# 78 products that nobody reads, at the head of an attention kernel: 36 and 42 beside TensorE's first transpositions

## The chip, the cores and the metric

The kernel runs on one core of a Trainium2 chip. The metric is the device time of one execution in microseconds; lower is better. Engines are called by their short names: PE is TensorE, DVE VectorE, ACT ScalarE, POOL GpSimd, SP the queue that issues most transfers.

## The reference, cut to what matters

Three layers in a row: block-causal attention, a top-1 mixture of experts with a capacity, and a noisy top-2 mixture of experts. Only the attention is touched.

```python
def _attn_ref(q, k, v):                      # 2 batches, 8 heads, 576 tokens, 64 wide
    scores = scale * np.matmul(q, k.transpose(0, 1, 3, 2))
    scores = np.where(mask, scores, -1e9)    # block_i >= block_j, blocks of 64
    attn = np.exp(scores - scores.max(-1, keepdims=True))
    attn = attn / (attn.sum(-1, keepdims=True) + 1e-09)
    return np.matmul(attn, v)

def reference(q, k, v, ...):
    x = rows_of(_attn_ref(q, k, v))          # 1152 x 512
    x = _moe_ref(x, ...)
    return _moe2_ref(x, ...)
```

## The kernel before, in words

The attention works on pairs of heads: 8 pairs `pr`, four for each batch. For a pair, `load_pair` (L319 to L324) brings q, k and v into SBUF; for the first pair q comes through SP's queue and k through ACT's. `turn_ops` then builds `w`, the transposed operand of the scores, in the tiles `both`. It has three parts:

- `main(x)`, once for q (`x == 0`) and once for k (`x == 1`): four transpositions on PE into one PSUM bank of the ring `tp` (L442), two ACT copies that round to fp32r (L450), and two DVE operations that keep the rest (L456 for q, L459 for k).
- `tail()`: the last 64 tokens of q and k by one product with a scaled identity (L479), two ACT copies (L487) and two DVE operations (L492).
- `dup`: copies to the other half of the partitions. For the first pair q's is done by ACT (L468) and k's by POOL (L470).

`tile_ops` follows: the scores (L526, L531) into the ring `s`, their maxima on DVE (L537, L540, L542), the exponentials on ACT (L550, L552), transpositions of the probabilities on PE (L562, L558, L565), copies back on ACT or DVE (L421, L423) and the products with v (L608, L623) into the bank `av`. At the head, DVE also copies the first pair's masks into the second pair's tile (L876).

Nothing of this is issued in the order in which it is written. `AT`, a `Weave`, collects operations with an engine, a cost and their dependences, and `run` simulates the engines with the costs given and issues each operation's instructions in the order that comes out. A function `pe(op)` is called when its operation's turn comes, so whatever it issues stands together in PE's queue, in front of whatever comes later. Each engine works through its own queue in order. The constant `ones` is a 128x128 bf16 tile that DVE sets to 1.0 at the program's start (L88); the attention's gates use it much later.

Of the kernel before, what the change touches and what calls it, by code (L numbers as in the profile page):

```python
# [46 lines left out]
def attention_moe_moe2(ctx, tc, q, k, v, wg1, w1a, w2a, cap, wg2, wn2, noise, w1b, w2b, out):  # L47
    nc = tc.nc
# [38 lines left out]
    ones = consts.tile([128, 128], BF, name="ones")  # L87
# [118 lines left out]
    class Weave:  # L206
# [80 lines left out]
        def bank(self, op, ring):  # L287
            return self.rings[ring][op["bank"][ring]]
# [8 lines left out]
    with ExitStack() as actx:  # L297
# [16 lines left out]
        def load_pair(b, p):  # L314
            qn, q4, vn = qns[(b * NP + p) % 2], q4s[(b * NP + p) % 2], vns[(b * NP + p) % 3]
            hs = slice(2 * p, 2 * p + 2)
            for i, src in enumerate((q, k)):
                for hh in range(2):
                    (nc.scalar if b == p == 0 and i == 1 else nc.sync).dma_start(out=qn[:, i, :, hh, :], in_=src[b, 2 * p + hh, 0:512, :].rearrange("(c p) d -> p c d", p=128))  # L319
            for i, src in enumerate((q, k)):  # L320
                nc.sync.dma_start(out=q4[64 * i:64 * i + 64], in_=src[b, hs, 512:576, :].rearrange("h p d -> p h d"))
            for hh in range(2):
                nc.sync.dma_start(out=vn[:, hh, 0:4, :], in_=v[b, 2 * p + hh, 0:512, :].rearrange("(c p) d -> p c d", p=128))
            nc.sync.dma_start(out=vn[0:64, :, 4, :], in_=v[b, hs, 512:576, :].rearrange("h p d -> p h d"))  # L324
# [78 lines left out]
        def store(b, c):  # L403
# [6 lines left out]
        rings = dict(s=pairs, big=big, p4=[P4], av=[psum.tile([128, 512], F32, name=f"av{i}") for i in range(RING["av"])],  # L410
                     tp=[psum.tile([128, 512], F32, name=f"tp{i}") for i in range(RING["tp"])],
                     pt=[work.tile([128, 512], F32, name=f"pt{i}") for i in range(RING["pt"])],
                     pT=[work.tile([128, 512], F32, name=f"pT{i}") for i in range(RING["pT"])],
                     xt=[work.tile([128, S], F32, name=f"xt{i}") for i in range(RING["xt"])])
# [9 lines left out]

        made = {}

        def load_op(pr):
            b, p = divmod(pr, NP)
            deps = [made.get(("tr", pr - 2, x)) for x in range(3)] + [made.get(("av", pr - 3))]
            made["load", pr] = AT.add("load", "S", 0.5, lambda op: load_pair(b, p), deps, dma=4.9)  # L430

        def turn_ops(pr):

            qn, q4, w = qns[pr % 2], q4s[pr % 2], W[pr % 2]
            used = made.get(("scores", pr - 2))
            res = []

            def main(x):
                C = [slice(64 * x * h, 64 * x * h + 512) for h in range(2)]
                def pe(op):  # L440
                    for t in range(4):
                        nc.tensor.transpose(bank(op, "tp")[:, 128 * t:128 * t + 128], qn[:, x, t].rearrange("p h d -> p (h d)"), ident)  # L442

                P = AT.add("tr", "P", 0.53, pe, [made["load", pr], used], ["tp"], shared=["tp"])
                made["tr", pr, x] = P

                def act(op):
                    for h in range(2):
                        o, c = HALF[h], C[h]
                        nc.scalar.activation(w[o, 2 * x, h, c], bank(P, "tp")[o], AF.Copy, scale=(0.125, 1.0)[x])  # L450

                def dve(op):
                    for h in range(2):
                        o, z, c = HALF[h], HALF[1 - h], C[h]
                        if x == 0:
                            nc.vector.scalar_tensor_tensor(w[z, 1, h, c], bank(P, "tp")[o], 0.125, w[o, 0, h, c].bitcast(F32),  # L456
                                                           op0=OP.mult, op1=OP.subtract)
                        else:
                            nc.vector.tensor_tensor(w[z, 2, h, c], bank(P, "tp")[o], w[o, 2, h, c].bitcast(F32), op=OP.subtract)  # L459

                def dup(op):
                    for h in range(2):
                        o, z = HALF[h], HALF[1 - h]
                        d = slice(0, 640) if x == 0 else slice(64 * h, 64 * h + S)
                        if pr:
                            nc.sync.dma_start(out=w[z, (0, 3)[x], h, d].bitcast(F32), in_=w[o, 2 * x, h, d].bitcast(F32))
                        elif x == 0:
                            nc.scalar.activation(w[z, 0, h], w[o, 0, h].bitcast(F32), AF.Copy)  # L468
                        else:
                            nc.gpsimd.tensor_copy(w[z, 3, h, d], w[o, 2, h, d].bitcast(F32))  # L470

                A = AT.add("hi", "A", 1.17, act, [P])
                V = AT.add("lo", "V", 1.4, dve, [P, A], frees=[(P, "tp")])
                res.extend([A, V])
                return dup, A

            def tail():
                def pe(op):
                    nc.tensor.matmul(bank(op, "tp")[:, 0:128], q4.rearrange("p h d -> p (h d)"), eighth, start=True, stop=True)  # L479

                P = AT.add("tr", "P", 0.26, pe, [made["load", pr], used], ["tp"], shared=["tp"])
                made["tr", pr, 2] = P

                def act(op):
                    for h in range(2):
                        o, c = HALF[h], TAIL[h]
                        nc.scalar.activation(w[o, 0:3:2, h, c], bank(P, "tp")[o, 0:128].rearrange("p (x n) -> p x n", x=2), AF.Copy)  # L487

                def dve(op):
                    for h in range(2):  # L490
                        o, z, c = HALF[h], HALF[1 - h], TAIL[h]
                        nc.vector.tensor_tensor(w[z, 1:3, h, c], bank(P, "tp")[o, 0:128].rearrange("p (x n) -> p x n", x=2),  # L492
                                                w[o, 0:3:2, h, c].bitcast(F32), op=OP.subtract)

                A = AT.add("hi", "A", 0.55, act, [P])
                V = AT.add("lo", "V", 0.6, dve, [P, A], frees=[(P, "tp")])
                res.extend([A, V])
                return A

            a2 = tail()  # L500
            for x in range(2):
                dup, A = main(x)
                if pr:
                    res.append(AT.add("dup", "G", 2.08, dup, [A, a2], dma=0.9))
                else:
                    res.append(AT.add("dup", "AG"[x], (1.48, 1.8)[x], dup, [A, a2]))
            made["W", pr] = res
# [362 lines left out]
        made["load", 0] = AT.add("load", "S", 0.0, lambda op: None, dma=6.0, lag=-3.6)  # L870
        turn_ops(0)
        load_op(1)
        def masks(h):
            o = HALF[h]
# [29 lines left out]
        for i in range(MORE):  # L904
            pr = B * NP - 2 + i
# [14 lines left out]
    rings = {n: [pp.tile([128, 512], F32, name=f"{n}{i}") for i in range(c)] for n, c in (("y", 2), ("h", 2), ("tp", 2), ("sm", 2))}  # L920
# [81 lines left out]
    def prep(F, rows, n, x, c0, deps=(), when=0.0, more=None):  # L1002

        xh, xl = x
        h = {}

        def tr(bank):
            h["tp"] = bank.rearrange("p (k n) -> p k n", n=128)
            for kk in range(KD):
                k = slice(kk * 128, (kk + 1) * 128)  # L1010
                if more:
                    nc.tensor.matmul(h["tp"][:, kk, :], rows()[:, k], ident, start=True, stop=False)
                    nc.tensor.matmul(h["tp"][:, kk, :], more[0][:, k], more[1], start=False, stop=True)
                else:
                    nc.tensor.transpose(h["tp"][:, kk, :n], rows()[:n, k], ident[:n, :n])  # L1015

        def hi():
            nc.scalar.activation(xh[:, :, c0:c0 + n], h["tp"][:, :, :n], AF.Copy)  # L1018

        def lo():  # L1020
            nc.vector.tensor_tensor(xl[:, :, c0:c0 + n], h["tp"][:, :, :n], xh[:, :, c0:c0 + n].bitcast(F32), op=OP.subtract)  # L1021

        t = F.add("P", 1.7 if more else 0.43 if n > 64 else 0.12, tr, deps, take="tp", after=when)
        a = F.add("A", 0.48 if n > 64 else 0.2, hi, [t])
        l = F.add("V", 0.6 if n > 64 else 0.2, lo, [a], frees=t, tail=F.par["prep"])
        return (l, t) if more else l
# [740 lines left out]
    x, t = prep(F, lambda: G[0, "early"][2], 128, xT[0], 128, deps=[d, m], more=(end[0], perm))  # L1767
# [47 lines left out]
```

## Time and profile before

| what | value |
|---|---|
| median of 3 runs | 550.33 us (548.28 to 551.72) |
| the profiled execution's own time | 548.57 us |
| its span, first to last instruction | 546.9 us |
| PE busy over the span | 514.3 us (94%) |
| DVE, ACT, POOL busy over the span | 378.8, 293.9, 139.7 us |
| PE busy in the first of 40 slices (13.7 us each) | 3 tenths; 9 tenths in most others |

1.7 us of the profiled execution's time lie outside its span. All times in the rows further below are counted from the span's start. In a timeline, instructions of one kind that follow each other are merged: the row has the start of the first, the time to the end of the last and their count. An idle time stands in brackets with what ended it, where there was any.

### The profile page before, as it was taken

What the parts mean: (1) busy time and instruction counts of PE and PEld (TensorE: products, weight loads), DVE (VectorE), ACT (ScalarE), POOL (GpSimd) and SP (SyncE); (2) the same over time, 40 slices, a digit from 0 to 9 for tenths busy, and PEclk for the clock granted to TensorE, in tenths of its full rate; (3) what the DMA queues carried; (4) which work ended last, traced back from release to release, by engine and by line L of the source; (5) the groups of instructions that cost most, each with busy time, mean ns of one, the idle gap of its engine ahead of it and who ended that gap; (6) DMA issues with size and microseconds to landing.
All of it is one profiled execution on the core that took longest, in us unless ns stands there. A gap on an engine that the chain in (4) does not pass through costs nothing. (4 is left out here: it accounts for less than half of the span.)

```text
span 546.9 us, 10105 instructions
## 1 busy us (share of the span) xinstructions
PE 514.3 (94%) x3381; PEld 421.5 (77%) x3381; DVE 378.8 (69%) x1008; ACT 293.9 (54%) x580; POOL 139.7 (26%) x225
## 2 busy tenths in 40 slices
PE   3999999999879999999999998999999999999996
PEld 3778777778646876796975976888889797789794
DVE  7899988898649888757675567637657492657441
ACT  5888878981347776643443346335536171726130
POOL 3000000000362344313423224114415051455021
PEclk9999999999999999999999999999999999999999
DMA  6988895523457788854632444528585775286120
GB/s 135 229 220 231 233 241 157 167 78 106 143 164 269 248 261 286 272 176 136 202 121 86 124 157 144 175 96 288 197 305 163 253 257 181 80 311 191 65 67 36
DMA packets 71176, 99.17 MB, mean 181 GB/s; under 512 B 37130, under 2 KB 40586, under 8 KB 71088
## 3 DMA queue, kind: packets, MB, share of 16 engines
q1 hardware_dynamic: 63600, 83.16, 48.3%
q0 software_dynamic: 6432, 14.71, 8.9%
q8 instruction: 39, 0.64, 0.5%
q14 instruction: 49, 0.40, 0.3%
q10 hardware_dynamic: 1056, 0.26, 0.2%
HBM read 87.53 MB, written 12.25 MB: 182 GB/s over the span
## 5 line engine op out<-in xcount | busy, mean ns | idle before, releaser
L170 DVE TENSOR_TENSOR wl<-raw,wh 128x512 fp32r<-128x512 f32 x140 | 91.5, 685 | 11.7 <-ACT wh L167 11.4
L167 ACT ACTIVATE wh<-raw 128x1024 fp32r<-128x1024 f32 x70 | 71.1, 1052 | 19.9 <-PEq L1779 12.5
L170 DVE TENSOR_TENSOR both<-raw,both 128x512 fp32r<-128x512 f32 x100 | 66.0, 685 | 9.0 <-ACT both L167 8.6
L167 ACT ACTIVATE both<-raw 128x1024 fp32r<-128x1024 f32 x50 | 51.4, 1055 | 10.0 <-PEq L1779 8.3
L198 PE MATMUL h<-xh,wh 128*128 128x256 f32 (+1 forms) x184 | 53.0, 288 | 0.6
L199 PE MATMUL h<-xl,wh 128*128 128x256 f32 (+1 forms) x184 | 52.5, 286 | 0.0
L200 PE MATMUL h<-xh,wl 128*128 128x256 f32 (+1 forms) x184 | 52.3, 284 | 0.0
L1018 ACT ACTIVATE xh<-tp 128x512 fp32r<-128x512 f32 (+1 forms) x37 | 18.9, 536 | 56.3 <-PE tp L1015 54.6
L1586 POOL DMA_INDIRECT out_dram<-o,T2i x16 | 18.6, 1165 | 99.8 <-DVE o L1583 97.6
L1021 DVE TENSOR_TENSOR xl<-tp,xh 128x512 fp32r<-128x512 f32 (+1 forms) x37 | 21.8, 610 | 31.1 <-ACT xh L1018 28.4
L1145 ACT ACTIVATE hh<-h 128x512 fp32r<-128x512 f32 (+1 forms) x46 | 24.1, 523 | 34.9 <-PE h L200 22.7
L198 PE MATMUL h<-xh,both 128*128 128x256 f32 (+1 forms) x136 | 39.2, 288 | 2.5 <-DVE hl L1148 1.2
L1148 DVE SCALAR_TENSOR_TENSOR hl<-h,hh 128x512 fp32r<-128x512 f32 (+1 forms) x46 | 27.4, 596 | 19.8 <-ACT hh L1145 15.1
L199 PE MATMUL h<-xl,both 128*128 128x256 f32 (+1 forms) x136 | 39.0, 287 | 0.0
L200 PE MATMUL h<-xh,both 128*128 128x256 f32 (+1 forms) x136 | 38.8, 285 | 0.0
L198 PE MATMUL y<-wh,hh 128*128 128x512 f32 (+1 forms) x94 | 38.3, 408 | 0.0
L200 PE MATMUL y<-wh,hl 128*128 128x512 f32 (+1 forms) x94 | 37.0, 394 | 0.0
L199 PE MATMUL y<-wl,hh 128*128 128x512 f32 (+1 forms) x94 | 36.9, 393 | 0.0
L526 PE MATMUL s<-both 128*128 128x256 f32 (+2 forms) x128 | 33.2, 372 | 3.8 <-ACT both L468 2.5
L550 ACT ACTIVATE pt<-s,negmax 128x128 f32<-128x128 f32 (+3 forms) x64 | 33.3, 525 | 6.3 <-DVE negmax L537 5.1
L198 PEld LDWEIGHTS h<-xh,wh 128*128 128x128 f32 x184 | 34.6, 188 | 2.2 <-issue 1.6
L1437 POOL MEMSET xr<- 128x524 f32 x3 | 1.5, 547 | 131.5 <-DVE T1f L811 131.5
(295 smaller groups left out, 1327.4 us busy)
## 6 DMA issues: line engine op xcount, KB each, us to landing
raw<-in_moe_w_dram SPq DMA_DIRECT2D x120, 512.0 KB, 5.3
wf<-in_moe_w_dram SPq DMA_DIRECT2D x8, 512.0 KB, 5.6
out_dram<-zero SPq DMA_DIRECT2D x3, 768.0 KB, 5.5
both<-both SPq DMA_DIRECT2D x14, 160.0 KB, 2.6
raw<-in_q_dram SPq DMA_DIRECT2D x16, 128.0 KB, 3.4
vn<-in_v_dram SPq DMA_DIRECT2D x16, 128.0 KB, 2.5
both<-both SPq DMA_DIRECT2D x14, 144.0 KB, 3.1
raw<-in_k_dram SPq DMA_DIRECT2D x14, 128.0 KB, 3.5
```

The costliest lines, as they stand in the source:

```text
L167: nc.scalar.activation(h, t, AF.Copy)
L170: (nc.gpsimd if part == 3 else nc.vector).tensor_sub(l[:, c], t[:, c], h[:, c].bitcast(F32))
L198: nc.tensor.matmul(o, sh, mh, start=first, stop=False)
L199: nc.tensor.matmul(o, sh, ml, start=False, stop=False)
L200: nc.tensor.matmul(o, sl, mh, start=False, stop=last)
L526: nc.tensor.matmul(o, w[:, i, h, 128 * t:128 * t + 128], w[:, i + 2, h, 64 * h:64 * h + n], start=(i == 0), stop=(i == 1))
L550: nc.scalar.activation(o, i, AF.Exp, bias=negmax[:, pr, 2 * t + h:2 * t + h + 1], accum_out=ssum[b][:, t, 2 * p + h:2 * p + h + 1])
L1018: nc.scalar.activation(xh[:, :, c0:c0 + n], h["tp"][:, :, :n], AF.Copy)
L1021: nc.vector.tensor_tensor(xl[:, :, c0:c0 + n], h["tp"][:, :, :n], xh[:, :, c0:c0 + n].bitcast(F32), op=OP.subtract)
L1145: nc.scalar.activation(part(hfull[0], g - (KF - 2 * WHOLE) // per) if plain(g) else part(hh, g), of(g), AF.Relu)
L1148: nc.vector.scalar_tensor_tensor(part(hl, g), of(g), 0.0, part(hh, g).bitcast(F32), op0=OP.max, op1=OP.subtract)
L1586: ins = nc.gpsimd.indirect_dma_start(out=out, out_offset=_off(G[key][1][:n, 0:1]), in_=G[key, "o"][:n], in_offset=None, bounds_check=NT - ...
```

## The change

A helper issues n products of `ones` with `ones` (128x128, bf16) into the first 128 columns of the only `av` bank. Each starts and stops its own accumulation, and nothing reads the result before the first product with v overwrites it. 36 are issued in the operation of the first pair's `main(0)`, ahead of its transpositions, and 42 in the operation of the first pair's `tail`, behind its product. Costs and dependences that the `Weave` sees are unchanged.

```diff
         made = {}
 
+        def unread(n):
+            for _ in range(n):
+                nc.tensor.matmul(rings["av"][0][:, 0:128], ones, ones, start=True, stop=True)
+
...
             def main(x):
                 C = [slice(64 * x * h, 64 * x * h + 512) for h in range(2)]
                 def pe(op):
+                    if pr == x == 0:
+                        unread(36)
                     for t in range(4):
                         nc.tensor.transpose(bank(op, "tp")[:, 128 * t:128 * t + 128], qn[:, x, t].rearrange("p h d -> p (h d)"), ident)
...
             def tail():
                 def pe(op):
                     nc.tensor.matmul(bank(op, "tp")[:, 0:128], q4.rearrange("p h d -> p (h d)"), eighth, start=True, stop=True)
+                    if pr == 0:
+                        unread(42)
```

What this makes of the order, on PE at the attention's head. Before, with the semaphores that each row waits for (`raw_72` is the first pair's q and k, `tp_204`, `tp_205` and `tp_206` are the three banks of the ring `tp`, `q_128` the last 64 tokens; DMAHW marks a transfer):

```order
L442 MATMUL tp_204<-ident,raw_72 128x128 [waits DMAHW4_49,DMAHW2_49,DVE_49]
L442 MATMUL tp_204<-ident,raw_72 128x128 x3
L442 MATMUL tp_205<-ident,raw_72 128x128 [waits DMAHW1_49,DMAHW0_49]
L442 MATMUL tp_205<-ident,raw_72 128x128 x3
L479 MATMUL tp_206<-eighth,q_128 128x128 [waits DMAHW5_49,DMAHW3_49,DVE_49]
L526 MATMUL s_201<-both_106 128x256 [waits DVE_49,Activation_49]
L526 MATMUL s_201<-both_106 128x256 [waits DVE_49,Pool_49]
```

The four rows into `tp_204` are k's, the four into `tp_205` are q's: DVE's first operation on `tp_204` is k's (L459), its first on `tp_205` is q's (L456). After the change, at the same place (lines below the helper have moved by 6 to 8; of the repeated pairs of rows of L429 the first stands for the 36, the second for the 42):

```order
L448 MATMUL tp_204<-ident,raw_72 128x128 [waits DMAHW4_49,DMAHW2_49,DVE_49]
L448 MATMUL tp_204<-ident,raw_72 128x128 x3
L429 LDWEIGHTS ones
L429 MATMUL av_203<-ones 128x128
...
L448 MATMUL tp_205<-ident,raw_72 128x128 [waits DMAHW1_49,DMAHW0_49]
L448 MATMUL tp_205<-ident,raw_72 128x128 x3
L485 MATMUL tp_206<-eighth,q_128 128x128 [waits DMAHW5_49,DMAHW3_49,DVE_49]
L429 LDWEIGHTS ones
L429 MATMUL av_203<-ones 128x128
...
L534 MATMUL s_201<-both_106 128x256 [waits DVE_49,Activation_49]
```

The 36 stand behind k's four transpositions, which wait for a transfer, and in front of q's four. The 42 stand between the tail's product and the first scores. The rows of all other engines' queues are the same before and after.

## Rows read from the trace of the kernel before

**Rows 1.** Busy time of each engine by stretch (second number: its length; x: instructions).

```profile
core 0: us, PE busy (x) PEld busy (x) DVE busy (x) ACT busy (x) POOL busy (x), PEclk, DMA share, GB/s
7.83:10.35 2.52, 0.01 (x2) 0.01 (x1) 2.43 (x5) 2.38 (x6) 1.32 (x2) 1.00 0.90 205
10.35:13.50 3.15, 2.47 (x9) 1.99 (x9) 3.02 (x7) 1.51 (x5) 0.00 (x0) 1.00 0.55 125
13.50:17.33 3.83, 3.83 (x16) 3.73 (x17) 1.81 (x4) 2.68 (x9) 0.00 (x0) 1.00 0.73 165
21.30:30.00 8.70, 7.51 (x66) 5.61 (x65) 7.99 (x17) 8.54 (x17) 0.00 (x0) 1.00 1.03 242
30.00:60.00 30.00, 29.64 (x264) 23.58 (x262) 28.56 (x65) 26.13 (x76) 0.00 (x0) 1.00 0.87 242
```

**Rows 2.** PE's timeline, 5 to 35 us.

```profile
5.47 1.94 PE L442 MATMUL tp<-ident,raw 128*128 128x128 f32 x8 [5.47 <-DMA raw<-in_k_dram]
7.20 0.63 PE L479 MATMUL tp<-eighth,q 128*128 128x128 f32 x2
10.35 2.47 PE L526 MATMUL s<-both 128*128 128x256 f32 x8 [2.51 <-ACT both L468]
13.50 1.01 PE L526 MATMUL s<-both 128*128 128x384 f32 x2 [0.68 <-DVE both L876]
...
14.72 1.06 PE L442 MATMUL tp<-ident,raw 128*128 128x128 f32 x4
15.58 0.63 PE L479 MATMUL tp<-eighth,q 128*128 128x128 f32 x2
16.00 1.06 PE L562 MATMUL tp<-ident,pt 128*128 128x128 f32 x4
16.72 1.35 PE L526 MATMUL s<-both 128*128 128x384 f32 x4
17.90 0.50 PE L562 MATMUL tp<-ident,pt 128*128 128x128 f32 x3
...
31.02 0.60 PE L652 MATMUL tp<-ident,xt 128*128 128x128 f32 x4
```

**Rows 3.** ACT's timeline, 6 to 21 us.

```profile
6.59 1.19 ACT L450 ACTIVATE both<-tp 64x512 fp32r<-64x512 f32 x2 [1.95 <-PE tp L442]
7.87 0.57 ACT L487 ACTIVATE both<-tp 64x128 fp32r<-64x128 f32 x2
8.46 1.21 ACT L450 ACTIVATE both<-tp 64x512 fp32r<-64x512 f32 x2
9.57 1.48 ACT L468 ACTIVATE both<-both 64x640 fp32r<-64x640 f32 x2
...
16.25 0.55 ACT L487 ACTIVATE both<-tp 64x128 fp32r<-64x128 f32 x2 [0.37 <-PE tp L479]
...
18.30 0.58 ACT L550 ACTIVATE pt<-s,negmax 128x384 f32<-128x384 f32 x1 [0.28 <-DVE negmax L540]
...
20.35 1.21 ACT L450 ACTIVATE both<-tp 64x512 fp32r<-64x512 f32 x2 [0.33 <-PE tp L442]
```

**Rows 4.** DVE's timeline, 0 to 22 us.

```profile
0.97 0.17 DVE L88 MEMSET ones<- 128x128 bf16 x1 [0.97 <-PEq L1798]
...
9.86 1.41 DVE L456 SCALAR_TENSOR_TENSOR both<-tp,both 64x512 fp32r<-64x512 f32 x2
11.29 0.85 DVE L876 CAST both<-both 64x640 fp32r<-64x640 f32 x2
```

**Rows 5.** PE's timeline, 11.74 to 12.9 us: the last scores of the first two tiles.

```profile
11.48 1.33 PE L526 MATMUL s<-both 128*128 128x256 f32 x5
```

**Rows 6.** PE's timeline around 132.8 us: bf16 products of 48 columns.

```profile
132.80 0.26 PE L806 MATMUL tp<-where,place 128*128 128x48 bf16 x4
```

**Rows 7.** PE's timeline, 450 to 454 us: products of 512 columns, one row each.

```profile
449.91 0.39 PE L199 MATMUL y<-wl,hh 128*128 128x512 f32 x1
450.14 0.39 PE L200 MATMUL y<-wh,hl 128*128 128x512 f32 x1
```

## The prediction

> **What bounds the kernel now.** I read the stretches first, then PE's timeline at the head, then ACT's and DVE's. The reader is to see three things.
>
> First, at the head the engines wait for each other in a chain. PE transposes k and q from 5.47 and ends the tail's product at 7.20 + 0.63 = 7.83 [rows 2]. ACT takes the tail (L487) at 7.87, q at 8.46 and q's copy at 9.57, with hardly a gap, and the first scores start at 10.35 when that copy's first half is done [rows 2, 3]. In that gap PE does nothing (0.01 of 2.52 us) while ACT is busy for 2.38 [rows 1]. From 9.86 DVE has q's rest and the mask copies and is busy for 3.02 of the next 3.15 us from 10.35 [rows 1, 4].
>
> Second, PE runs at its lower level there. The page's granted clock says 1.00 in every stretch, but the durations say otherwise: four transpositions took 1.06 us at 14.72 and at 16.00, and 0.60 at 31.02; three took 0.50 at 17.90 [rows 2]. [...] Ahead of the rise PE had been busy without a gap for 3.83 us, from 13.50 [rows 1]; the 2.47 us busy from 10.35, which an idle stretch of 2.51 preceded and one of 0.68 followed, had brought no rise [rows 2].
>
> Third, behind the head the binding engine is ACT from 21.3 to 30 (8.54 of 8.70 us, PE 7.51), then PE (29.64 of 30.00 from 30 to 60) [rows 1]. No long idle time lies there in which a late head could vanish, so what the head loses or gains is passed on to the end, nearly one to one. PE as a whole is 94% busy.
>
> **The change part by part.** Only PE's queue changes. The two additions are priced one by one.
>
> *One unread product.* No row before has a 128-column bf16 product back to back. [...] I take 0.057 at the high and 0.11 at the low level. The weight load of each should not show: bf16 products of 48 columns, each with its load, fit four into 0.26 us, the last one's whole length included [rows 6]. Bounds: below, less than 0.07, which is 0.26 / 4; above, the 0.21 us from one fp32 transposition of 128 columns to the next at the low level, (7.20 - 5.47) / 8 [rows 2], and half of that at the high.
>
> [...]
>
> *The 36.* They don't stand in front of the first transpositions: k's four come first and wait for k's transfer until 5.47, so the 36 can't use the idle time before it. k's four are issued by 5.47 + 4 x 0.216 = 6.33; then q's four and the tail's product wait behind 36 x 0.11 = 3.96 us, at the low level. Behind the 36 stand, on PE, q's transpositions and the tail; on ACT L487, L450 for q and L468, in that order; on DVE L492, L456 and the mask copies; on POOL L470. All of them move. Only k's first copies (6.59 on ACT) and their rest on DVE stay.
>
> Against this, PE is then busy without a gap from 5.47, and I expect its clock to rise much earlier. By the one stretch that brought it, the earliest is 5.47 + 3.83 = 9.30. I place the rise at the end of the 36, about 10.3. q's transpositions and the tail then cost 0.60 + 2 x 0.11 = 0.81 us instead of 1.50 (6.33 to 7.83) [rows 2]. The tail is 3.96 - 0.69 = 3.27 us late. Bounds: a rise at 9.30 leaves 27 products at 0.11 and 9 at 0.057, and the tail is 2.8 late; one after only 2.47 us (7.94) leaves 2.1; one after q's transpositions leaves 3.96.
>
> [...]
>
> *The 42.* They fill the time in which ACT works. Their cover runs from the tail's last issue (7.20 + 2 x 0.21 = 7.62) to the first scores at 10.35: 2.73 us, moved as a whole. At the high level they take 42 x 0.057 = 2.4 us and cost nothing. At 0.11 they take 4.6 and cost 1.9. Their cover is gone from 2.73 / 42 = 0.065 us a product.
>
> *What the faster clock gives back.* Between 10.35 and 17.33 PE was busy for 2.47 + 3.83 = 6.3 us at the low level [rows 1]; at the high one that is 3.15 less. Not all of it lies on the path. Up to 16 us the path runs through DVE and ACT. After it ACT waited for PE's work three times: 0.37 at 16.25, 0.28 at 18.30 (DVE's maximum was behind a copy that waited for PE) and 0.33 at 20.35 [rows 3]; then ACT binds. With PE twice as fast these 0.98 us close, and no more, since an engine can't be earlier than its own work. Bounds: 0 and 3.15; I take 0.98, the nearest rows.
>
> *The sum.* 3.27 + 0 - 0.98 = +2.3 us. The profiled execution took 548.57 us (546.9 of span and 1.7 outside), so on its own base 550.9. The median of the three runs, 550.33, lies 1.8 above that execution; on it the sum is 552.6, and that is what I name, since medians are compared. It is 0.4% slower; a measurement of this kernel tells about 1% from no change.
>
> **Rivals.**
>
> 1. *All of PE's saved time counts.* For it: PE is 99% busy from 30 us on. Against: from 21.3 to 30 ACT is, and PE has idle time. Then 3.27 - 3.15 = +0.1: 550.4 us.
>
> 2. *An unread product takes twice as long, because its weight load is not hidden* (the slower side). For it: the fp32 transpositions of 128 columns stand 0.21 apart. Against: the 48-column products with their loads. With a rise at 9.30, 14 products at 0.213 and 22 at 0.11 end at 11.72, the tail at 12.53: 4.7 late; the 42 take 4.6 and stand out by 1.9; less 0.98 that is +5.6: 555.9 us, just over 1%. It decides from 0.065 us a product at the high level.
>
> 3. *The clock does not rise before the scores.* For it: I know of one rise, and busy time at 10.35 had brought none. Against: the 36 leave PE no gap. Then 3.96 + 1.9 and nothing given back: +5.9, 556.2 us.
>
> 4. *The change does what its title says, and the 36 run during the wait before 5.47.* `ones` is there from 0.97 + 0.17 = 1.14 [rows 4], so they would end at 1.14 + 3.96 = 5.1. k's copies would start 0.46 earlier and 0.98 be given back: 548.9 us. The order speaks against it.
>
> **How the numbers follow.** Forecast (a delay of 2.1 to 3.96, with 0.5 to 1.5 given back): 0.65, its own range 551.0 to 553.8. Rival 1: 0.15. Rival 2: 0.08. Rival 3: 0.08. Rival 4: 0.02. Something else: 0.02. The range takes in rival 1 less the spread of the runs (550.4 - 1.3 = 549.1) and rival 3 (556.2). Rivals 2 and 3 lie at the bound of 1%, about half beyond it: slower 0.09 with something else; faster 0.02; within 1% 0.89.
>
> **What would show it.** In the profile after: k's transpositions still at 5.47; 36 products behind them, 0.11 us apart, up to about 10.3; L495 on ACT (L487 before) at about 11.1 instead of 7.87; the 42 ended before the first scores, which start near 13.6; no transposition at the 1.06 length after it; ACT's idle times of 0.37, 0.28 and 0.33 gone; at 30 us and later everything some 2.3 us later. It would be wrong if the 42 end behind ACT's L474, if the first scores start before 12 or behind 15 us, or if the shift of 2 to 3 us is found at 30 us but not at the end.

## The result, and the profile after

The changed kernel takes 556.65 us (median of 6 runs, 554.41 to 561.26), the kernel before, on the same chip, 550.1 us (median of 6, 548.28 to 551.72). The ratio is 1.0124, with a 95% interval of [1.0086, 1.0162]; a ratio is taken over all runs and can differ by up to 0.2% from that of the medians. The forecast was 552.6, the range 549.1 to 556.2: the result lies 0.45 above the range, and beyond the 1% that tells from no change, where "slower" had a chance of 0.09.

The profiled execution took 556.87 us. From its page: the span, the clock in 40 slices, and the queue q8, named "instruction" (packets, MB, share; before it had 39 packets).

```profile
span 555.1 us, 10261 instructions
...
PEclk9999999999999999999999997999999999999999
...
q8 instruction: 41, 0.67, 0.5%
```

The span is 8.2 us longer than before (546.9). One slice of the clock stands out, the 25th (333 to 347 us), far from the attention's head. Head first: PE's timeline, which answers to [rows 2].

```profile
5.57 1.09 PE L448 MATMUL tp<-ident,raw 128*128 128x128 f32 x4 [5.57 <-DVE both L346]
6.45 4.05 PE L429 MATMUL av<-ones 128*128 128x128 bf16 x36
10.29 1.03 PE L448 MATMUL tp<-ident,raw 128*128 128x128 f32 x4
11.15 0.40 PE L485 MATMUL tp<-eighth,q 128*128 128x128 f32 x2
11.38 2.51 PE L429 MATMUL av<-ones 128*128 128x128 bf16 x42
14.06 0.54 PE L534 MATMUL s<-both 128*128 128x256 f32 x2 [0.17 <-ACT both L474]
...
31.25 1.20 PE L534 MATMUL s<-both 128*128 128x256 f32 x8
...
334.87 0.73 PE L1353 MATMUL sm<-C,S 128*128 128x144 f32 x4 [0.68 <-DVE C L1348]
336.21 0.41 PE L1251 MATMUL tp<-ident,px 128*128 128x128 f32 x2 [0.61 <-DVEq L1537]
338.74 0.64 PE L1251 MATMUL tp<-ident,px 128*128 128x128 f32 x2 [2.12 <-issue]
339.03 0.78 PE L198 MATMUL h<-wh,xh 128*128 128x512 f32 x1
339.60 0.63 PE L199 MATMUL h<-wl,xh 128*128 128x512 f32 x1
345.85 0.40 PE L198 MATMUL h<-wh,xh 128*128 128x512 f32 x1
```

The head is as forecast. The 36 stand behind k's transpositions, 0.107 us apart ((10.29 - 6.45) / 36), and PE goes over to its higher level about 11.2, by the durations alone, since the page's granted clock reads 1.00 on both sides: the four transpositions at 10.29 still take 1.03 us, the tail's pair at 11.15 takes 0.40 where it took 0.63. The 42 take 2.51 us, 0.060 each, end at 13.89 and are hidden: the first scores wait 0.17 us more, for ACT.

ACT's timeline, which answers to [rows 3]:

```profile
11.58 0.57 ACT L495 ACTIVATE both<-tp 64x128 fp32r<-64x128 f32 x2 [3.69 <-PE tp L485]
...
19.29 0.55 ACT L495 ACTIVATE both<-tp 64x128 fp32r<-64x128 f32 x2
...
21.08 0.58 ACT L558 ACTIVATE pt<-s,negmax 128x384 f32<-128x384 f32 x1
...
23.01 1.21 ACT L456 ACTIVATE both<-tp 64x512 fp32r<-64x512 f32 x2 [0.21 <-PE tp L448]
```

The tail's copies start 3.71 us late (11.58 against 7.87), and of ACT's three idle times two are gone and one is 0.21. At its row L456 the delay is 23.01 - 20.35 = 2.66, so 1.05 us have been given back.

The rest of the loss is late, in a part that the change doesn't touch. The same place in the trace of before, PE's timeline:

```profile
331.64 0.73 PE L1345 MATMUL sm<-C,S 128*128 128x144 f32 x4 [0.68 <-DVE C L1340]
333.07 0.63 PE L1243 MATMUL tp<-ident,px 128*128 128x128 f32 x4 [0.71 <-DVEq L1529]
...
333.77 0.39 PE L199 MATMUL h<-wl,xh 128*128 128x512 f32 x1
...
337.53 0.40 PE L198 MATMUL h<-wh,xh 128*128 128x512 f32 x1
```

Up to 334.87 the delay is 3.23 us (334.87 - 331.64). Then, behind the `If` of L1537, PE does two of four transpositions, stops for 2.12 us with nothing that the profile shows to wait for ("issue"), and does the other two. Behind the stop a product of 512 columns takes 0.63 instead of 0.39. The stretches of after show why (columns as in [rows 1]; the eighth value is the granted clock):

```profile
core 0: us, PE busy (x) PEld busy (x) DVE busy (x) ACT busy (x) POOL busy (x), PEclk, DMA share, GB/s
138.00:140.00 2.00, 2.00 (x11) 2.00 (x11) 1.97 (x5) 0.00 (x0) 0.00 (x0) 0.50 0.24 64
336.00:338.80 2.80, 0.47 (x3) 0.27 (x4) 1.76 (x4) 0.79 (x1) 2.17 (x5) 1.00 0.01 3
338.80:345.70 6.90, 6.90 (x22) 5.80 (x23) 3.89 (x16) 2.76 (x5) 1.13 (x1) 0.51 0.44 138
```

From 338.8 to 345.7 PE runs at half the clock (0.51). Between the first transposition (336.21 against 333.07) and the thirteenth product of 512 columns behind it (345.85 against 337.53) the delay grows from 3.14 to 8.32 us; 2.12 of that are the stop, about 3 go with the lower clock. At the end 8.2 are left. A second stop of this kind, 1.06 us at 264.84, had raised the delay from 2.1 to 3.2. The stretch at half the clock at 138 had not lasted: the delay was 4.1 behind it and 2.2 at 155 us.

So of 8.2 us in this execution about 2.5 belong to the head (2.46 at 100.96, where the same scores start at 98.50 before). The question for the runs: why does PE stop at 336?

### The profile page after: what moved, and what is told of

Same layout as the page of the kernel before. It is cut to its first block, busy times and chain, and to the rows that moved or that the text cites. A ratio compares the mean times of both kernels' runs of the same rounds, so it can differ in the third digit from the quotient of the medians.

```text
span 555.1 us, 10261 instructions
## 1 busy us (share of the span) xinstructions
PE 522.3 (94%) x3459; PEld 429.3 (77%) x3459; DVE 379.1 (68%) x1008; ACT 293.6 (53%) x580; POOL 140.6 (25%) x225
## 5 line engine op out<-in xcount | busy, mean ns | idle before, releaser
L199 PEld LDWEIGHTS h<-xl,wh 128*128 128x128 f32 x184 | 34.6, 188 | 0.0
```

The costliest lines, as they stand in the source:

```text
L199: nc.tensor.matmul(o, sh, ml, start=False, stop=False)
```

## The experiments

Two theories. **Layout**: the page has one queue of 16384-byte packets named "instruction" (0.64 MB in 39 before). The change puts 156 more instructions into PE's program (10261 in its profile against 10105: 78 products, each with a weight load), which moves all that PE executes later against the borders of these pieces; behind some jumps PE then waits for a piece, and behind the stop its clock falls. **Shift**: the late loss follows from the head's being 2.6 us late, which makes transfers and engines meet differently. The theories part on a kernel that has the instructions and not the products, and on one that has the products and another number of instructions. For that, the runs use empty PE instructions:

```diff
+        def pad(n):
+            for _ in range(n):
+                nc.tensor.nop(hint="pad", nofuse=True)
```

"x added" below means x PE instructions more than before, products (two each) and empty ones together.

**156 empty instructions, no product.** Before, with `pad(56)` ahead of k's first transpositions and `pad(20)` ahead of the tail's product in each of pairs 1 to 5.

> The kernel before with 156 empty instructions on PE at the attention's head (56 ahead of k's transpositions, 20 in each of the next five pairs) and no unread product: as many instructions as the change adds. Layout theory (the late 5.5 us come from where the later code lies in the pieces of 16384 bytes in which PE's instructions are fetched): the head stays as before, PE stops near 262 us for about 1 us and near 334 us for about 2 us with nothing to wait for, its clock falls behind that, and the median is 552 to 556. Shift theory (the late loss comes from the head ending 2.6 us later): none of this, 549 to 551.5.

Measured: 555.01 us against 550.24, ratio 1.0078 [1.0049, 1.0107]. PE's timeline:

```profile
267.94 0.29 PE L200 MATMUL h<-xh,wl 128*128 128x288 f32 x1 [1.16 <-issue]
...
339.18 0.41 PE L1251 MATMUL tp<-ident,px 128*128 128x128 f32 x2 [0.55 <-DVEq L1537]
341.70 0.69 PE L1251 MATMUL tp<-ident,px 128*128 128x128 f32 x2 [2.10 <-issue]
342.03 0.78 PE L198 MATMUL h<-wh,xh 128*128 128x512 f32 x1
```

Both stops are there, at the same two instructions and of the same length to within 0.1 us, and behind the second the long product runs at 0.78 again. No product was added and the head is only 0.4 to 1.0 us late. So the stops came with the 156 instructions. The execution in the profile was the slowest of seven (560.85 us; the other six took 554.29 to 555.77), so its total is not the typical one: it has a third stop, of 1.66 us at 199.42, and two more stretches at half the clock, from 156.0 to 162.9 and from 200.4 to 203.8 us (products of 512 columns take 0.63 us there, 0.39 outside).

**The change and 100 empty instructions (256 added).** 256 instructions are taken to be one piece, so that the later code stands against the borders as before. This is an estimate from the traces: in the kernel before, packets on q8 start at 29.34 and, seven packets later, at 125.46 us, and in between PE has 834 products and 836 weight loads, 239 for each packet; in the change it has 977 and 975 over eight packets (20.59 to 133.71), 244 for each. PE's other instructions are not in these counts. All seven kernels with 256 added have 40 packets, one more than before. The other 50 stand in the tails of pairs 1 to 5, ten in each.

```diff
+                    if pr == 0 and x == 1:
+                        pad(50)
                     if pr == x == 0:
                         unread(36)
```

> The changed kernel with 100 empty instructions more, so that PE has 256 instructions more than before, one piece of 16384 bytes. Layout theory: the head is 2.6 us late as in the changed kernel, no stop of 2 us near 337, 551.5 to 553.5. Shift theory: 556 to 557, as the changed kernel.

Measured: 551.06 us, ratio 1.0028 [1.0001, 1.0054]: 5.6 us less than the change itself, with 100 instructions more. PE's timeline:

```profile
6.29 3.08 PE L433 MATMUL av<-ones 128*128 128x128 bf16 x36
...
335.67 0.63 PE L1259 MATMUL tp<-ident,px 128*128 128x128 f32 x4 [0.64 <-DVEq L1545]
336.06 0.48 PE L198 MATMUL h<-wh,xh 128*128 128x512 f32 x1
```

No stop. Here the rise came earlier, inside the 36 (3.08 us for them), so the head was late by only 1.15 us at 20, and by 1.2 from 30 to 134 us; the change's was 2.5. So some 1.3 of the 5.6 us are a lighter head.

**256 empty instructions, no product (the control).** Before, with `pad(56)` in front and `pad(40)` in the tail of five pairs.

> The kernel before with 256 empty instructions and no unread product: what the padding itself costs. Both theories: 549 to 551.5, no stop of PE over 1.3 us that before does not have. Over 552 the padding has a price of its own and the other padded kernels are read against this one.

Measured: 557.99 us, ratio 1.0157 [1.0103, 1.0212]. Not what was expected, and not for either theory: the late stops are gone, but the 40 in a row cost time where they stand, 1.5 to 2.0 us in each of pairs 2 to 5.

```profile
32.72 0.46 PE L487 MATMUL tp<-eighth,q 128*128 128x128 f32 x2 [1.60 <-issue]
```

All of its delay is there by 83 us and doesn't grow afterwards. So this control is lost for the sum, but not for the stops. A pad must be cut small and put where PE waits anyway.

**The 36 really in front of k's transpositions, 256 added.** Two tries at what the title suggests; the first with `pad(50)` ahead of the 36, the second with `pad(2)` and the rest spread over seven pairs.

```diff
+                    if pr == 0 and x == 1:
+                        pad(2)
+                        unread(36)
```

> The 36 moved in front of k's transpositions, where the title puts them, the 42 unchanged, 100 empty instructions as above. Layout theory: k's transpositions still start near 5.5, at the high clock, the first scores some 0.5 us earlier than before, about 1 us more given back by 25 us: 548 to 550. Shift theory: the same. A rival: the 36 end behind 5.5 and the head is late by 0.5 to 1: 550 to 552.

Measured: 552.11 us, ratio 1.0021 [0.9995, 1.0047], and no test of the place: the 36 started only at 4.62, behind the empty instructions.

> The 36 in front of k's transpositions again, but the empty instructions (100, to make one whole piece of 16384 bytes) nearly all moved to the later pairs, so that PE is free from 1 us on (in the first try 50 of them held PE's queue until 4.6). Theory that the 36 pay where they fill the wait: they run from 1.2 to about 5.1, the clock is up at k's transpositions or shortly behind, first scores near 10.0 instead of 10.35, head at 25 us some 1.0 to 1.5 earlier than before, median 548.5 to 549.5. Rival (the head gains nothing that lasts): 550 to 551.

Measured: 551.86 us against 549.21, ratio 1.0031 [1.0000, 1.0061]. PE's timeline:

```profile
1.19 3.71 PE L433 MATMUL av<-ones 128*128 128x128 bf16 x36 [1.19 <-DVE ones L88]
...
10.01 1.97 PE L544 MATMUL s<-both 128*128 128x256 f32 x8 [0.73 <-ACT both L482]
...
29.98 0.50 PE L544 MATMUL s<-both 128*128 128x256 f32 x2 [2.33 <-DMA both<-both]
...
33.05 1.06 PE L670 MATMUL tp<-ident,xt 128*128 128x128 f32 x4
```

The 36 end at 4.9, 0.75 us before k's transpositions can start, and the scores start 0.34 earlier than before. At 18 us the head is 1.17 us early. It doesn't last: at 29.98 the second pair's scores wait 2.33 us for the transfers of its copies (`both<-both`), and this kernel is now 1.4 us later than before. SP issued the last two of these copies at 22.03 and 22.60, where before they were issued at 21.00 and 21.62, although the head was early: one load ahead of them in its queue (L321) took 2.02 us to issue instead of 0.60. Why it did isn't shown. Behind the wait PE's clock fell, too, from 31.7 to 35.1: the four transpositions at 33.05 take 1.06 us where they took 0.60 at 31.02, and from 36 us on the delay is 2.9. So here the lead was lost at the next transfers, and more than the lead. The two starts also give an estimate of an empty instruction, (4.62 - 1.19) / 48 = 0.071 us, if nothing else held the 36 in the first try.

**Each part alone, 256 added.** Only the 42, only the 36, and 72 with the 42.

> The 42 alone behind the tail, padded by 172 empty instructions to one piece. By the prediction's prices: 42 products from 7.6 at 0.11 us until the clock rises (about 9.3 to 11), then 0.058, end between 10.8 and 12; first scores 0.4 to 1.7 late; then about 1 us given back: 549.7 to 551. Rival (the 42 bring no early rise): first scores 1.9 late and nothing given back, 552.

Measured: 551.49 us against 549.21, ratio 1.0037 [1.0000, 1.0074].

```profile
7.53 3.56 PE L433 MATMUL av<-ones 128*128 128x128 bf16 x42
10.89 1.25 PE L542 MATMUL s<-both 128*128 128x256 f32 x8
...
29.86 1.52 PE L542 MATMUL s<-both 128*128 128x256 f32 x5 [1.94 <-DMA both<-both]
```

At the lower level at first (3.56 us for them, 2.51 in the change), the 42 stand out of their cover by 0.54 us, the scores then run at the high level (1.25 for eight against 2.47), and the head is 0.99 early at 18 us. It loses that to the same transfers (issued at 21.52 and 22.09), and its clock is at half from 30.2 to 37.0 (1.06 us for four transpositions at 33.25): from 36 us on it is 3.8 late.

> The 36 alone between k's and q's transpositions, padded to one piece. Theory (the 36 are the head's whole cost, the 42 are covered): first scores 2 to 3.7 us late, 0.9 to 1.5 given back by 25 us as in the changed kernel, median 551 to 552.5, like the padded changed kernel (551.06). Rival (the 42 keep the clock up over the wait for ACT): without them the clock falls or does not rise, nothing given back, 553 to 554.

Measured: 552.59 us against 549.21, ratio 1.0048 [1.0021, 1.0075].

```profile
13.86 2.41 PE L542 MATMUL s<-both 128*128 128x256 f32 x8 [2.52 <-ACT both L482]
...
18.09 1.06 PE L456 MATMUL tp<-ident,raw 128*128 128x128 f32 x4
```

The tail's pair at 10.96 had taken 0.39, so PE was at the higher level. Without the 42 PE is then idle for 2.52 us and the scores are back at the lower level, 2.41 for eight; so are the transpositions at 18.09. Of the 3.51 us by which the tail's copies are late (11.38 on ACT) 3.46 are left at 28 us. So in the change the 42 kept PE at the higher level for the give-back.

> 72 instead of 36 between k's and q's transpositions, 42 unchanged, padded by 28 to one piece. Theory: the second 36 run at the high clock, 36 x 0.057 = 2.1 us more on the head's path than the padded changed kernel (551.06): 552.5 to 553.8. Rival (the delay is absorbed behind the head): 551.

Measured: 552.94 us against 549.21, ratio 1.0051 [1.0025, 1.0078].

```profile
6.47 6.51 PE L433 MATMUL av<-ones 128*128 128x128 bf16 x72
12.82 0.61 PE L454 MATMUL tp<-ident,raw 128*128 128x128 f32 x4
```

Twice the products between the transpositions make the head 4.78 us late at 24 us, 2.1 more than in the change, which is 36 x 0.06. This is the latest head of all, and no stop stands near 265 or 340: at 338.10 the four transpositions run on, 0.63 us for them, and the delay of 4.6 us at 134 is 5.3 at the end. So here a late head alone brought no stop, which speaks against the shift theory.

**Other numbers of instructions.** The change with `pad(16)` in front (172 added), with 30 behind the tail instead of 42 (132 added), and 24 behind the tail alone (48 added).

> The changed kernel with only 16 empty instructions more on PE (172 instead of 156). Layout theory in its sharp form: in the changed kernel a piece of 16384 bytes ends only a few instructions behind a place to which PE jumps (near 336 us), so that the next piece is fetched too late; 16 instructions more put that end ahead of the jump's target. Then the stop of 2.1 us in the middle of four transpositions is gone, and with it the fall of the clock behind it, and the median is 551.5 to 553.5. Rival (any addition that is not a whole piece does harm in the same way): 555 to 557.

Measured: 563.59 us against 550.0, ratio 1.0240 [1.0214, 1.0265]. The stops grew, where this sharper form of the layout theory had wanted them shorter or gone:

```profile
345.04 0.89 PE L1257 MATMUL tp<-ident,px 128*128 128x128 f32 x4 [3.02 <-issue]
```

The stop now stands ahead of the first transposition, the four that follow are together, and the clock is at half (0.50) from 345.3 to 352.1. Of the 3.02 us 0.71 are a wait that stands at this place before the change, too (333.07). The profile has more stops than the change's, among them 2.06 us at 165.01, 0.92 at 200.84 and 2.91 at 267.64.

> 36 and 30 products, 132 instructions, no empty ones. The end of the piece then lies 24 instructions further behind the jump's target than in the changed kernel, and the fetch has some 2 us more. Layout theory: the stop near 336 is under 0.7 us; median 551 to 553.5. Rival (the stop comes with the products' number or with the late head): 556.

Measured: 554.08 us against 550.0, ratio 1.0058 [1.0036, 1.0080]. The four transpositions follow each other without a stop, and one of 1.00 us stands further on:

```profile
338.87 0.63 PE L1255 MATMUL tp<-ident,px 128*128 128x128 f32 x4 [0.55 <-DVEq L1541]
...
339.80 0.40 PE L200 MATMUL h<-wh,xl 128*128 128x512 f32 x1
341.20 1.04 PE L1264 MATMUL sm<-wcat,x2t 128*128 128x16 f32 x8 [1.00 <-ACT both L167]
```

> 24 products behind the tail alone (48 instructions, none empty, no 36): the version that the earlier runs point to. At the low clock they end inside ACT's work (24 x 0.107 = 2.6 of 2.7 us), so the first scores stay at 10.35; the clock is up near 10 to 12 and about 1 us is given back by 22 us, of which the transfers of the second pair may take some back near 28. If no piece ends badly: 548.5 to 550, at best a little under the kernel before; if one does: 551 or more, with a stop of PE of 1 to 2 us to be seen.

Measured: 550.38 us against 550.0, ratio 1.0005 [0.9980, 1.0030]. The head is 1.0 us early at 17 us and 0.4 late at 29, behind a wait of 0.79 us for the second pair's transfers: no gain. No stop stands near 333. No version was faster than the kernel before.

**A test of the refined theory: 36 and 36 (144 added).** Laid side by side, the runs so far showed that a stop wanders through the code as instructions are added, and that it ends about the same time, 2.53 to 2.77 us, after a packet of 16384 bytes starts on the instruction queue. That was put to one more count.

> The change with 36 products behind the tail instead of 42: 144 instructions more than before, halfway between 132 and 156. Theory, layout, in its refined form: each stop of PE near 335 to 345 us ended 2.5 to 2.8 us after a packet of 16384 bytes began on the queue that brings instructions, and it stood later in the code the fewer instructions were added: with 132 behind the third product that follows the four transpositions, with 156 behind the second transposition, with 172 ahead of the first. So with 144 it stands between: behind the third or fourth transposition or behind the first or second product, 1.1 to 2.1 us long, and the next instruction starts 2.5 to 2.8 us after the packet. Time 552 to 557. Rival, shift: the stop goes with how late the head is, which is the same as in the change to within 0.4 us; then it is 2.1 us long again, in the middle of the four transpositions, or none. A third way, chance: a stop in another place, or one whose end does not lie 2.5 to 2.8 us behind such a packet.

Measured: 551.56 us against 549.99, ratio 1.0036 [1.0016, 1.0056]. PE's timeline:

```profile
6.36 3.44 PE L433 MATMUL av<-ones 128*128 128x128 bf16 x36
...
334.87 0.63 PE L1255 MATMUL tp<-ident,px 128*128 128x128 f32 x4 [0.55 <-DVEq L1541]
...
335.80 0.40 PE L200 MATMUL h<-wh,xl 128*128 128x512 f32 x1
337.43 1.04 PE L1264 MATMUL sm<-wcat,x2t 128*128 128x16 f32 x8 [1.23 <-ACT both L167]
```

The stop has left the four transpositions, is 1.23 us long and ends 2.45 us after the packet. It stands one product later than expected, in the same place as with 132, and 2.45 is just under the 2.5 that was named. The 2.1 us or nothing of the rival is not there. The row names ACT, but the copy that this product needs (L1259) had ended at 336.18; the wait is not for it.

How the packet's start is read: the DMA view of a stretch of 0.2 us around it, here 335.9 to 336.1 us of the changed kernel, holds one packet on that queue and no other.

```profile
DMA packets 1, 0.02 MB, mean 82 GB/s; under 512 B 0, under 2 KB 0, under 8 KB 0
...
q8 instruction: 1, 0.02, 40.9%
```

The place between 333 and 345 us, by the number of instructions added (times in us; where there is no stop, two columns are empty):

| added | kernel | packets on q8 | packet starts | PE goes on | apart | stop | where it stands |
|---|---|---|---|---|---|---|---|
| 0 | before | 39 | 333.58 | | | none | |
| 132 | 36 and 30 | 40 | 338.67 | 341.20 | 2.53 | 1.00 | behind the third product |
| 144 | 36 and 36 | 40 | 334.98 | 337.43 | 2.45 | 1.23 | behind the third product |
| 156 | the change | 41 | 336.00 | 338.74 | 2.74 | 2.12 | behind the second transposition |
| 156 | empty ones alone | 41 | 339.03 | 341.70 | 2.67 | 2.10 | behind the second transposition |
| 172 | the change and 16 | 41 | 342.39 | 345.04 | 2.65 | 3.02 | ahead of the first |
| 256 | the change and 100 | 40 | 336.27 | | | none | |

The other stops end alike: 2.61 us after a packet at 262.23 in the change, 2.71 after one at 265.23 and 2.64 after one at 196.78 in the kernel of 156 empty instructions, and 2.77, 2.69 and 2.54 after packets at 162.24, 198.15 and 265.10 with 172. None of the other kernels with 256 has a stop near 340. So, as these runs are best read, PE waits for a fetch that starts about 0.2 us or less from the first transposition behind the jump (336.00 and 336.21, 338.67 and 338.87, 334.98 and 334.87), and what it can do meanwhile would be the code between the jump's target and the next border: the four transpositions and three products with 132, two transpositions with 156, nothing with 172.

What the traces show of this are packets of 16384 bytes, and 2.45 to 2.77 us from the packet's start to the next instruction; the branch itself is in no row, and that PE waits for the packet was not shown.

## Why the prediction was wrong

**What bounds the head, and the order.** Right. The 36 stand behind k's transpositions, ACT's tail copies and the first scores move together by 3.71 us (11.58 against 7.87, 14.06 against 10.35), and a place in front of them (rival 4) would not have paid: 551.86.

**The price of one product.** Right: 0.107 us at the low level (forecast 0.11) and at most 2.51 / 42 = 0.060 at the high (0.057), the last one's own length included. No run shows the 0.11 and 0.057 themselves; the runs showed 0.107 and 0.060 in their place. They were the author's estimates: 0.057 is a quarter of the 0.23 us between the products of [rows 7], 0.11 a little under half of what one of 256 columns takes in [rows 5] (1.33 / 5 = 0.27).

**The 36: 3.27 us.** It was 3.71, inside the bounds of 2.1 to 3.96. The rise came at 11.2, behind q's transpositions, and not at the end of the 36. When it comes varies, and the "earliest" of 9.30 was no bound: with 100 empty instructions it came inside the 36, at about 8.2 (3.08 us for them), and with 36 and 36 at about 9.0 (3.44 us). In the other direction, with 156 empty instructions, where PE does the same work at the head as before, four scores at 16.88 took 1.84 us, still at the low level, where they took 1.35 at 16.72. So a size inside these bounds was partly luck.

**The 42: nothing.** Right, and they did more than was said: without them (36 alone) PE was back at the lower level behind the gap of 2.52 us, 2.41 us for eight scores, and only 0.05 us were given back.

**The give-back: 0.98.** It was 1.05, most of it at the three waits named. The net of the head was 2.66 us at 23 us, 2.64 at 31.25 (28.61 before) and 2.46 at 100.96 (98.50 before), against 2.3.

**"So what the head loses or gains is passed on to the end, nearly one to one", and "Only PE's queue changes".** Here it failed. The first held for the head's own delay. The second was the error: the sum priced the 156 instructions by how long PE is busy with them, and put what they do to the instructions behind them at nothing, without a reason. That term was 1.06 + 2.12 us of stops and about 3 us of the lower clock (0.51) from 338.8 to 345.7; with small gains elsewhere it makes 5.7 of the 8.2 us in the profiled execution. The prediction's own sign, a shift of 2 to 3 us at 30 us that is not found at the end, came in. In medians the change costs 6.5 us. Without the late stops it costs 0.8 (551.06 against 550.24, 256 added, with a head 1.3 us lighter), with one stop of 1.23 us it costs 1.6 (551.56 against 549.99, 144 added, six products fewer). The 156 empty instructions cost 4.8 (555.01 against 550.24), about 1 of it ahead of the first stop. So an estimate from these is that 4 to 6 of the 6.5 us are the layout's.

**The rivals.** Rival 3's 556.2 is near the result for another reason: PE did reach the higher level, at 11.2, before the scores at 14.06. Rival 2's product of twice the price isn't there (0.060), nor is rival 1's gain.

**Left open.** The border of a piece is in no row of a trace, nor is the branch, so where a stop will stand is known only in order (more instructions, earlier in the code), and 144 was off by a product. At the stops of 2.1 us and more near 340 the clock fell in each of the three profiles (to 0.51, 0.50 and 0.50); behind those of 1.0 to 1.2 us it did not (1.00 with 144; with 132 a product of 512 columns still took 0.39 us). Elsewhere it fell at one of 2.91 us (267.64, with 172; 0.50 up to 273.6) and at one of 1.66 (199.42, with 156 empty ones; 0.63 us for a product of 512 columns), and did not at one of 2.06 (165.01, with 172; 1.00 up to 172). That the stop is the cause of the fall is argued from that, not shown, and other stretches at half the clock (137.4 to 140.9 in the change, 0.51) have no such stop ahead of them.

## What to carry to other kernels

Here a change that adds 156 instructions to one engine, in a program with `If`s, had a second price far from where it is made, by the estimate above 4 to 6 of 6.5 us. For another change of this kind: read the instruction queue's packets, and look behind each jump for waits for "issue", or for an engine that had long been done, before the local sum is believed. To tell the two prices apart, put the same number of empty instructions without the work, and the work with the count filled up to a whole piece (here 256). A stretch of work that nobody reads would have paid here only with its own delay hidden and the lead it gives not waited away at the next transfer. In the change the first didn't hold, in the runs with the 36 in front, the 42 alone and the 24 alone the second didn't; after the two longer of those waits (2.33 and 1.94 us) the clock was lost as well.

## What was not expected of the hardware

- Behind one jump PE's idle time grew from 0.7 to as much as 3.0 us with the number of instructions far ahead of it: 555.01 us with 156 empty ones and no product, against 550.24; with products too 550.38 with 48 added, 556.65 with 156, 563.59 with 172, 551.06 with 256.
- An empty PE instruction was not free: 40 in a row left PE idle for 1.4 to 1.6 us at three places, and an estimate from two starts is 0.071 us each.
- PE was back at the lower level behind one gap of 2.52 us (36 alone: 1.06 us for four transpositions), and in the change 6.9 us at half the clock (0.51) cost about 3 us, more than the stop of 2.12 ahead of them.
